# A sigmoid-attention and SwiGLU kernel: issue order from a list scheduler, scores in bursts of two, row tails loaded per batch, last stores on SyncE

## The chip, the cores and the metric

One core of one Trainium2 chip. The metric is the device time of one launch in microseconds (us). Faster or slower asks for 2%.

## The reference

```python
# q, k, v: (batch 8, heads 12, seq 448, head_dim 64)
scores = scale * np.matmul(q, k.transpose(0, 1, 3, 2)) - np.log(448)
attn = 1.0 / (1.0 + np.exp(-scores))          # a sigmoid, no softmax
x = np.matmul(attn, v)                        # -> (3584 tokens, 768)
g = x @ w_gate                                # 768 x 1536
silu = g * (1.0 / (1.0 + np.exp(-g)))
out = silu * (x @ w_val) @ w_out              # 1536 x 768
```

## The kernel before

Work is cut into 24 units of four heads of one batch; three units make a batch. A unit's attention is: transposes of q and k (`emit_tr`, twice), seven score products into double banks of PSUM with a sigmoid on ScalarE for each, and two PV products (`emit_pv`). The FFN runs three units behind: a block is a gate and a value product of six matmuls (`emit_f1`), and output products (`emit_f2`) come once two batches are through. The rows 384 to 447 of each head, the "row tails", are loaded apart. (PSUM is where the kernel has its matmuls write; PV is the product of the sigmoids with v.) Everything is issued in the order written; each engine works through its own queue in that order. The scores have two buffers (tag `A`), the transposes and output products share one (tag `TO`).

```python
def emit_sc(i, pp, s):                       # one score pair: two 64-row tiles side by side
    sc = psum.tile([128, 2, 512], FP32, tag="A", bufs=2, name="ps_sc")
    ...
# the loop over units i and four slots sl (cut)
if f1:
    gps = emit_f1(fb, ff, wg16, "ps_g")
    t1 = emit_gate_post(gps)
if sl == 0:
    jobs = [emit_sc(i, 0, 0), emit_sc(i, 0, 1)]
elif sl == 1:
    jobs = [emit_sc(i, 0, 2), emit_sct(i)]
elif sl == 2:
    jobs = [emit_sc(i, 1, 0), emit_sc(i, 1, 1)]
else:
    jobs = [emit_sc(i, 1, 2)]
...                                          # PV of (i-1, 1) in slot 0, of (i, 0) in slot 3
for jb in jobs:
    emit_sig(jb)
...
if i + 1 < NQ and sl in (1, 2):
    emit_tr(i + 1, sl - 1)
if f1:
    vps = emit_f1(fb, ff, wv16, "ps_v")
...                                          # then an output product, casts, loads
```

The loads of a unit bring q, k, v in 384 KB each and its tails in four small transfers of 256-byte rows; all stores are issued from GpSimd.

## Time and profile before

| before | |
|---|---|
| time, median | 479.8 us |
| TensorE busy | 95% of a span of 479.3 us |
| first score sigmoid starts | 10.98 us |
| 21st sigmoid starts (the last that three units need) | 32.16 us |
| first gate matmul starts | 34.42 us |
| last matmul starts / span ends | 473.0 / 479.3 us |

"Half clock" below is a stretch in which the profile's clock record grants TensorE 0.5, or in which matmuls start twice as far apart as later.

The prediction below shows the lines on TensorE. One view it only tells of is ScalarE's, in the timeline of the start (start and length in us, engine, line, what, count; in brackets the idle time before and what ended it):

```profile
19.28 2.80 ACT L188 ACTIVATE pt<-ps_sc,sbiast 128x896 f16<-128x896 f32 x3 [1.23 <-PE ps_sc L174]
...
22.85 5.63 ACT L188 ACTIVATE pt<-ps_sc,sbiast 128x896 f16<-128x896 f32 x6
...
30.37 4.75 ACT L188 ACTIVATE pt<-ps_sc,sbiast 128x896 f16<-128x896 f32 x5 [0.99 <-PE ps_sc L174]
```

Sigmoids run in rows of three to six without a hole, 0.93 to 0.95 us each (a row's length by its count). From the first to the 21st start 21.2 us pass, of which 20 at 0.935 us are 18.7: holes of 2.5 us in all (the idle times that the view prints add up to 2.6).

I also use one measure of my own. For each moment I take the time minus a fixed length for each matmul started until then: 187 ns for 448 columns, 160 ns for 384, 53 ns for a transpose, two half tiles side by side counted once. These are set just under the distances between starts in the full stretch, whose medians are 189, 162 and 56 ns. The result is TensorE time lost so far, whether to waits, to the half clock or to changes of tile mode.

### The profile page before, as it was taken

To read this page: it belongs to the slowest core of one execution; us is meant where nothing else is said; L and a number is where in the kernel's file an instruction comes from. 1 tells how busy PE (TensorE), PEld (TensorE's weight loads), DVE (VectorE), ACT (ScalarE), POOL (GpSimd) and SP (SyncE) were. 2 spreads that over 40 slices of the span, in tenths; PEclk is the share of its full clock that TensorE was granted. 3 is DMA by queue.
4 is the path that set the end of the run, shared out by engine and by line. 5 is a ranking of instruction groups with operands and counts; after the bars stand their busy time and mean duration, and the time that the engine had idled before them with its cause. 6 is when DMAs were issued, how large, how long until landed. Compare 5 with 4: busy or idle time off the path is not lost.

```text
span 479.3 us, 7353 instructions
## 1 busy us (share of the span) xinstructions
PE 455.2 (95%) x2832; PEld 223.6 (47%) x2832; DVE 207.1 (43%) x421; ACT 221.0 (46%) x295; POOL 125.0 (26%) x216
## 2 busy tenths in 40 slices
PE   2886999999999999999999999999999999999995
PEld 1332444444445544444444454454454544554562
DVE  3342555555444344444444445444544443433210
ACT  3883556566554445454554544454454462112110
POOL 2777677322130023311311033023210000000010
PEclk9997999999999999999999999999999999999998
DMA  8999999963414045144234033220000001010032
GB/s 233 307 340 327 330 333 332 260 182 106 115 52 133 0 149 148 42 142 115 82 100 117 34 120 92 85 83 36 33 2 33 34 34 33 21 46 34 33 100 98
DMA packets 68578, 58.67 MB, mean 122 GB/s; under 512 B 22208, under 2 KB 65216, under 8 KB 68544
## 3 DMA queue, kind: packets, MB, share of 16 engines
q1 hardware_dynamic: 66240, 47.20, 33.7%
q0 software_dynamic: 2304, 11.01, 6.3%
q8 instruction: 22, 0.36, 0.3%
q14 instruction: 12, 0.10, 0.1%
HBM read 47.19 MB, written 11.01 MB: 121 GB/s over the span
## 4 chain that ended last, share of the span: by engine, by line
PE 88%; DMA 6%; SPq 1%; issue 1%; DVE 1%; ACT 1%; POOL 0%; POOLq 0%
PE ps_g L218 23%; PE ps_v L218 22%; PE ps_o L250 16%; PE ps_ol L250 7%; PE ps_sc L174 7%; PE ps_pv L198 6%; PE ps_tr L153 3%; DMA st_k<-in_k_dram 3%; PE ps_pv L200 3%; PE ps_sct L182 2%; DMA st_wg<-in_moe_w_gate_dram 1%; DMA st_q<-in_q_dram 1%; DMA sv<-in_v_dram 1%; DVE t L226 1%; SPq L98 1%
## 5 line engine op out<-in xcount | busy, mean ns | idle before, releaser
L188 ACT ACTIVATE pt<-ps_sc,sbiast 128x896 f16<-128x896 f32 x144 | 138.7, 1004 | 2.5 <-PE ps_sc L174 2.5
L224 ACT ACTIVATE s<-ps_g 128x448 f16<-128x448 f32 x96 | 52.1, 543 | 168.7 <-PE ps_g L218 168.7
L218 PE MATMUL ps_g<-xT,wg 128*128 128x448 f16 x576 | 125.8, 355 | 0.8 <-DVE t L226 0.8
L218 PE MATMUL ps_v<-xT,wv 128*128 128x448 f16 x576 | 125.8, 355 | 0.0
L226 DVE TENSOR_TENSOR t<-ps_g,s 128x448 f16<-128x448 f32 x96 | 60.0, 625 | 148.2 <-ACT s L224 148.2
L250 PEld LDWEIGHTS <-hT 128*128 128x128 f16 x672 | 64.5, 98 | 48.2 <-DVE kbd L163 4.9
L218 PEld LDWEIGHTS <-wg 128*128 128x128 f16 x576 | 56.6, 98 | 52.8 <-issue 3.4
L250 PE MATMUL ps_o<-wo,hT 128*128 128x384 f16 x456 | 80.5, 327 | 0.0
L218 PEld LDWEIGHTS <-wv 128*128 128x128 f16 x576 | 54.9, 98 | 42.3 <-issue 1.3
L233 DVE SCALAR_TENSOR_TENSOR hT<-ps_v,t 128x448 f16<-128x448 f32 x96 | 60.0, 625 | 32.4 <-PE ps_v L218 28.8
L263 POOL DMA_DIRECT2D out_dram<-osb x24 | 13.2, 552 | 230.7 <-DVE osb L255 115.0
L174 PE MATMUL ps_sc<-qkT 64*128 64x448 bf16 x288 | 46.1, 368 | 2.9 <-ACT pt L188 2.6
L198 PE MATMUL ps_pv<-pt,v 128*64 128x448 f16 x288 | 37.0, 365 | 0.0
L250 PE MATMUL ps_ol<-wo,hT 128*128 128x384 f16 x216 | 35.9, 326 | 0.0
L160 DVE COPY qkT<-ps_tr 128x832 bf16<-128x832 bf16 x48 | 28.2, 588 | 17.0 <-PE ps_tr L156 17.0
L207 DVE CAST xT<-ps_pv 128x448 f16<-128x448 f32 x48 | 30.0, 625 | 12.7 <-PE ps_pv L200 11.0
L122 POOL CAST v<-st_v 128x768 f16<-128x768 f32 x24 | 19.8, 826 | 49.6 <-PE ps_pv L198 38.0
L153 PE MATMUL ps_tr<-idn,k 128*128 128x128 bf16 x144 | 17.0, 230 | 13.4 <-ACT k L120 6.2
L253 ACT ACTIVATE osb<-ps_o 128x384 f32<-128x384 f32 x19 | 9.3, 490 | 43.9 <-PE ps_o L250 43.9
L174 PEld LDWEIGHTS <-qkT 64*128 64x128 bf16 x288 | 10.8, 95 | 37.9 <-issue 37.5
L188 ACT ACTIVATE pt<-ps_sct,sbiast 128x896 f16<-128x896 f32 x24 | 24.2, 1010 | 0.1
L122 POOL CAST q<-st_q 128x768 bf16<-128x768 f32 x23 | 18.9, 823 | 19.0 <-issue 12.1
(36 smaller groups left out, 225.1 us busy)
## 6 DMA issues: line engine op xcount, KB each, us to landing
st_q<-in_q_dram SPq DMA_DIRECT2D x24, 384.0 KB, 4.8
st_k<-in_k_dram SPq DMA_DIRECT2D x24, 384.0 KB, 5.0
st_v<-in_v_dram SPq DMA_DIRECT2D x24, 384.0 KB, 4.0
out_dram<-osb POOLq DMA_DIRECT2D x24, 384.0 KB, 2.6
st_wg<-in_moe_w_gate_dram SPq DMA_DIRECT2D x12, 384.0 KB, 5.4
st_wv<-in_moe_w_val_dram SPq DMA_DIRECT2D x12, 384.0 KB, 6.5
st_wo<-in_moe_w_out_dram SPq DMA_DIRECT2D x12, 384.0 KB, 5.6
sqk<-in_q_dram SPq DMA_DIRECT2D x24, 64.0 KB, 3.3
```

What stands on the lines that cost most here:

```text
L122: eng.tensor_copy(out=o, in_=i)
L153: nc.tensor.transpose(out=ps[:, off + s * 128:off + (s + 1) * 128], in_=src[:, s, hs, :], identity=idn)
L160: nc.vector.tensor_copy(out=m, in_=ps[:, mo:mo + S + SM])
L174: nc.tensor.matmul(out=sc[:, hp, 0:S], lhsT=kT[r, s * 128:(s + 1) * 128], rhs=qT[r, :], start=True, stop=True)
L188: nc.scalar.activation(out=pt, in_=sc[:, :, 0:S], func=SIGM, bias=sb_t, scale=qkscale)
L198: nc.tensor.matmul(out=pv[c, :], lhsT=v16[i][:, 2 * pp + hp, s, :], rhs=pts[(i, pp, s)][:, hp, :], start=(s == 0), stop=False)
L207: nc.vector.tensor_copy(out=t, in_=pv)
L218: nc.tensor.matmul(out=ps, lhsT=w[c][:, j, ff * 128:(ff + 1) * 128], rhs=xT[(b, j)], start=(j == 0), stop=(j == KC - 1))
L224: nc.scalar.activation(out=s16, in_=gps, func=SIGM)
L226: nc.vector.tensor_tensor(out=t1, in0=gps, in1=s16, op=MULT)
L233: nc.vector.scalar_tensor_tensor(out=hT[(m, f)][:, o * S:(o + 1) * S], in0=vps, scalar=HSC, in1=t1, op0=MULT, op1=MULT)
L250: nc.tensor.matmul(out=o, lhsT=hT[(m, f)][:, t * 128:(t + 1) * 128], rhs=wo16[f][:, cs], start=(f == 0), stop=(f == NF - 1))
```

## The change

Its intent: fill TensorE's holes in the start by an order that knows when data come, and spend less on mode changes. Each step becomes an `Op` with an engine, an assumed duration, what it waits for, and buffers that it takes and gives. A list scheduler walks through assumed time and lets each engine take the first ready step among the next 40 (TensorE), 12, 16, 8 or 1; the program is then issued in order of the assumed starts. Below, the diff is cut and regrouped.

```diff
+LAT = {"PE": 0.2, "ACT": 0.1, "DVE": 0.08, "POOL": 0.12, "SP": 2.2}
+SWITCH = 0.1
+DMA_RATE = 330e3
+def list_schedule(ops, bufs, window):
 ...  (cut)
+            for o in q[:window.get(e, 1)]:
+                r = ready(o)          # None while a buffer that it takes isn't free
 ...
+    def burst(i, ds):
+        def fpe():
+            for pp, s in ds:
+                sc = psum.tile([128, 2, 512], FP32, tag="A", bufs=2, name="ps_sc")
 ...
+        a = op("PE", 0.19 * len(ds), fpe, deps=[R["qkT", i, pp] for pp, _ in ds],
+               mode=("R", "R"), take=["A"] * len(ds))
 ...
-                    jobs = [emit_sc(i, 0, 0), emit_sc(i, 0, 1)]
+                            burst(i, ((0, 0), (0, 1)))        # slot 0
-                    jobs = [emit_sc(i, 0, 2), emit_sct(i)]
+                        burst_tail(i)                         # slot 1
-                    jobs = [emit_sc(i, 1, 0), emit_sc(i, 1, 1)]
+                        burst(i, ((0, 2), (1, 0)))            # slot 2
-                    jobs = [emit_sc(i, 1, 2)]
+                        burst(i, ((1, 1), (1, 2)))            # slot 3
 ...
+            if (i + 3) % QB == 0:
+                tails_batch((i + 3) // QB)     # tails of three units in four transfers
 ...
+        dma = nc.sync if final else nc.gpsimd  # last stores; the very last one in halves,
+                                               # its eviction split over ScalarE and VectorE
+    window = {"PE": 40, "ACT": 12, "DVE": 16, "POOL": 8, "SP": 1}
+    for o in list_schedule(ops, slots, window):
+        o.fn()
```

A dummy activation loads the sigmoid table at once, unit 0's q, k and v are loaded and cast in halves, and FFN blocks are dealt out three per unit at first and up to five later. The matmuls are the same.

## The prediction

> **What bounds the kernel now.** I read the page first, parts 1 and 2: which engine is full, and where along the span it isn't.
>
> ```profile
> PE 455.2 (95%) x2832; PEld 223.6 (47%) x2832; DVE 207.1 (43%) x421; ACT 221.0 (46%) x295; POOL 125.0 (26%) x216
> ...
> PE   2886999999999999999999999999999999999995
> ...
> ACT  3883556566554445454554544454454462112110
> ...
> PEclk9997999999999999999999999999999999999998
> DMA  8999999963414045144234033220000001010032
> ```
>
> A slice is 12 us. From slice 4 (48 us) to the end TensorE is full, and no other engine is. Only three things can shorten the run: the first 48 us, less TensorE time for the same products, and the last microseconds after TensorE. In the first slices ACT is full in slices 1 and 2, and the DMA engines are full in slices 1 to 7, so those two limit the start.
>
> Next, the timeline of the start (start, length, engine, line, what; in brackets the idle time and what ended it):
>
> ```profile
> 9.68 1.28 ACT L188 ACT_TABLE_LOAD   x1 [3.49 <-PE ps_sc L174]
> 10.98 2.80 ACT L188 ACTIVATE pt<-ps_sc,sbiast 128x896 f16<-128x896 f32 x3
> ...
> 34.42 1.30 PE L218 MATMUL ps_g<-xT,wg 128*128 128x448 f16 x6
> ...
> 40.80 0.50 PE L153 MATMUL ps_tr<-idn,k 128*128 128x128 bf16 x3 [4.30 <-POOL k L122]
> ...
> 41.52 2.45 PE L218 MATMUL ps_v<-xT,wv 128*128 128x448 f16 x6
> ...
> 47.20 1.30 PE L218 MATMUL ps_v<-xT,wv 128*128 128x448 f16 x6
> ```
>
> The reader is to see four losses. The first score sigmoid runs at 10.98, after a table load that waited for the scores. The first FFN block starts at 34.42, when the 21 sigmoids of three units are through (ACT from 10.98 to 33.2, with about 1.5 us of holes: it paces this stretch). Then TensorE stands 4.30 us, because the next instruction in program order is a transpose of unit 4, whose k has only just been loaded and cast, while products for unit 3 and the FFN were to be had. And after that hole it runs at half clock: 2.45 us for six matmuls, later 1.30.
>
> Then the steady state, TensorE alone:
>
> ```profile
> 203.23 1.30 PE L218 MATMUL ps_g<-xT,wg 128*128 128x448 f16 x6
> 204.46 0.36 PE L174 MATMUL ps_sc<-qkT 64*128 64x448 bf16 x2
> 204.76 0.55 PE L182 MATMUL ps_sct<-qkT,kbd 128*128 128x448 bf16 x2
> 205.14 0.33 PE L153 MATMUL ps_tr<-idn,k 128*128 128x128 bf16 x3
> ```
>
> Starts count here, not lengths. Six full matmuls take 1.14 from start to start (the chain of waits prints 1.14), but before a 64-row score pair they take 1.23; the pair, two matmuls side by side worth 0.19, takes 0.30 until the full-array tail score. A change between full array and half tiles costs about 0.10 us each time. Per unit I count 4 entries into scores, 2 exits to full array, 2 from scores to the column-tiled PV, 2 from there to full array: 10 changes, about 1.1 us.
>
> Last, the end:
>
> ```profile
> 443.59 1.29 PE L218 MATMUL ps_g<-xT,wg 128*128 128x448 f16 x6 [0.16 <-DVE t L226]
> ...
> 473.42 0.56 DVE L255 TENSOR_SCALAR osb<-ps_ol 128x384 f32<-128x384 f32 x1 [3.34 <-PE ps_ol L250]
> ...
> 474.53 0.54 POOL L263 DMA_DIRECT2D out_dram<-osb  x1 [3.35 <-issue]
> ```
>
> Late FFN blocks with nothing between them wait 0.16 us per gate or value bank. After the last matmul 0.56 us of scaling, 0.55 us until the store's descriptor starts on GpSimd, 0.54 us of issue, and a landing (2.6 us in the table of DMA issues) make up the end at 479.3.
>
> **What the Trainium skill says.** "TensorEngine Tiling (Array Packing)", Key Properties: changing the tiling mode drains TensorE. The trace agrees, with the 0.10 us per change above. "TensorE: Matmul & The Clock Gate", Part 1: the clock falls to half after an idle window of about 3.4 us and comes back after a busy one of that length. The trace agrees: a 4.30 us hole, then 2.24 us per six matmuls in the chain for 4.5 us, then 1.14. "ScalarE: Activation LUTs", What ACT_TABLE_LOAD costs: about 1283 ns plus a drain; here the load took 1.28 us and no drain of that size shows before the sigmoid at 10.98. "DMA: Bandwidth & Descriptors", Why small descriptors are slow: transfers in 256-byte pieces lose bandwidth. The row tails are such pieces; in the stretch 14 to 18 us, in which two units' tails move, the engines are 0.95 busy at 231 GB/s, against 340 to 360 when weights move.
>
> **The change part by part.** No arithmetic goes away; the matmuls are the same, so TensorE's own work stays.
>
> (a) Start. TensorE's work up to 46.14, when it is full and at full clock, at full-rate durations: transposes 9 x 0.41 = 3.7, score pairs 21 x 0.19 = 4.0, tail scores 4 x 0.38 = 1.5, PV 6 x 0.88 = 5.3, three FFN halves 3.4, mode changes about 3.5: 21.4 us. So 46.1 - 21.4 = 24.7 us are lost before it is full.
> After the change: the sigmoid table is loaded by a dummy activation at once (1.28 us off the path), and q and k of unit 0 come in halves. Against that the row tails of three units come ahead of it, 0.39 MB for q/k where the first unit needed 0.13, in 256-byte pieces. In the trace the first tails were cast at 6.08; I put the new ones 1 us later, so transposes at 7, copy 0.6, scores at 8.2, first sigmoid at 8.7 instead of 11.0. Then 21 sigmoids at 0.94 (3 in 2.80) = 19.7 us plus the old 1.5 us of holes and 0.5 for bursts that need both score buffers: 30.4; PV and its cast 1.3: FFN from about 31.5 instead of 34.4. The 4.3 us hole and the half clock after it (2.3 us) should go, since the list order puts ready work first: three FFN blocks wait on the first weight chunk, whose casts ended at 26.7 in the trace. By 31.5 TensorE has done about 16.5 us of work, so 15 are lost. Gain 9.5 us. DMA check: 330 GB/s bring units 0-2, chunk 0, unit 3, chunk 1, unit 4 (11.8 MB) at about 38 to 41 us; work then in hand (3 blocks of 2.27, unit 3 of 4.9) lasts until 43. It is close, so I allow 1 us of waits: **-8.5 us**.
>
> (b) Three score bursts of two instead of 2, 1, 2, 1. One entry and one exit fewer per unit, 0.2 us, in 21 units past the start: 4.2 us, if the list order keeps PV behind its burst. If it separates them, one change comes back per burst and nothing is gained. I take **-3 us**.
>
> (c) Order in the steady state. The page has 14 waits of the output product's weight load on the key-block copy, 4.9 us together, some 0.13 us of it visible in the matmul starts each time (1.27 instead of 1.14 before ps_o): 2 us. The late bank waits: about 1 us. The scheduler may fill half: **-1.5 us**.
>
> (d) Stores. The last evictions are split over ACT and DVE (0.56 to about 0.35), the last store is halved and issued from SyncE, which drops the 0.55 us before the descriptor: **-1 us**. Of the other stores nothing is on the path. Fewer tail DMAs (24 x 4 to 8 x 4 issues of 0.6 us) free SyncE, but the DMA engines were full in the start anyway: 0.
>
> Sum: -14 us. 479.8 - 14 = **465.8 us**, 2.9% faster.
>
> **The rivals.** First: DMA is the true bound up to 96 us, and the earlier FFN start only meets the weights earlier. For: 1.02 to 1.12 DMA share from 20 us on, and the 4.3 us hole ended with a load. Against: TensorE had no hole from 46 us on, though it did four FFN blocks per unit with loads in the same order; the new order asks for three. If true, half of (a) is lost: about 470. Second: the static order is a queue, and where the schedule's durations differ from the chip's (it assumes 330 GB/s from the first byte, and no half clock) TensorE waits at the head for something late while ready work stands behind it. Each wait over 3.4 us costs clock as well. Likely in the first 50 us only; it would give 468 to 473. Third: two scores per burst need both score buffers, so ACT runs dry between bursts. In the steady state ACT needs about 10 us of a unit's 14 to 20, so it has room; in the start it would cost about 0.4 us per burst, 9 bursts, part of which I took. Fourth, the other way: filling TensorE with the next unit's scores and PV brings the start's loss to 10 us, total about 460.
>
> **Range and chances.** The start carries most of the spread (gain 3 to 13 us), the bursts 0 to 4.5, the rest 1 to 4. Taken together 458 to 473. The 2% line is 470.2 us; only when the start gives less than 4 or 5 us is it missed. Faster 0.80, within 2% 0.18, slower 0.02.
>
> **What would show it.** First sigmoid at 8 to 9.5 us; first gate matmul at 30 to 33; no TensorE hole over 3 us after it and full granted clock from there; TensorE full from then to the end. Per unit three score entries and eight mode changes, 13.8 us per unit with four FFN blocks and no output product, against 13.97 now. The end 1 us nearer to the last matmul. Wrong if the transposes or the gate still wait on casts of late loads after 31 us, if PV stands apart from its burst everywhere, or if new waits on score buffers cut into the full stretch.

## The result, and the profile after

The changed kernel takes 474.28 us (median of 4, 474.1 to 474.78) beside 479.8 us for the kernel before (4 runs); the ratio is 0.9886 with an interval from 0.9869 to 0.9904. It is 1.1% faster, within 2%, where 2.9% was foretold.

The page of the changed kernel, busy times and slices (11.8 us each):

```profile
PE 451.4 (96%) x2832; PEld 224.0 (47%) x2832; DVE 205.1 (43%) x422; ACT 221.9 (47%) x296; POOL 120.5 (26%) x207
...
PE   2778999999999999999999999999999999999996
...
ACT  3577666656445354453554455445545344121111
...
PEclk9979999999999999999999999999999999999999
DMA  8999999989413253332541323000000001110032
```

Against the page of before, TensorE's first four digits are 2, 7, 7, 8 as against 2, 8, 8, 6: the start is hardly better filled. ScalarE, which was at 8 in slices 1 and 2, is at 5 and 7. The half clock is still there, one slice earlier.

ScalarE's timeline in the start:

```profile
8.96 1.91 ACT L385 ACTIVATE pt<-ps_sc,sbiast 128x896 f16<-128x896 f32 x2 [4.58 <-PE ps_sc L362]
12.87 1.01 ACT L385 ACTIVATE pt<-ps_sct,sbiast 128x896 f16<-128x896 f32 x1 [2.00 <-PE ps_sct L376]
15.12 1.91 ACT L385 ACTIVATE pt<-ps_sc,sbiast 128x896 f16<-128x896 f32 x2 [1.24 <-PE ps_sc L362]
18.80 1.91 ACT L385 ACTIVATE pt<-ps_sc,sbiast 128x896 f16<-128x896 f32 x2 [1.77 <-PE ps_sc L362]
21.89 1.91 ACT L385 ACTIVATE pt<-ps_sc,sbiast 128x896 f16<-128x896 f32 x2 [1.19 <-PE ps_sc L362]
...
32.54 1.01 ACT L385 ACTIVATE pt<-ps_sct,sbiast 128x896 f16<-128x896 f32 x1 [2.12 <-PE ps_sct L376]
```

The first sigmoid is 2 us earlier, as foretold (8.96, foretold 8.7). Then they come in twos, with a hole of 1.2 to 2.1 us before most of them, each ended by a score product. The 21st starts at 37.90: 28.9 us after the first, with 10.2 us of holes where there had been 2.5.

TensorE's timeline:

```profile
30.83 0.50 PE L336 MATMUL ps_tr<-idn,k 128*128 128x128 bf16 x3 [0.80 <-POOL k L199]
...
31.55 0.95 PE L376 MATMUL ps_sct<-qkT,kbd 128*128 128x448 bf16 x2
...
40.51 1.30 PE L424 MATMUL ps_g<-xT,wg 128*128 128x448 f16 x6
```

The first gate comes at 40.51, not at 31.5, and 6 us later than before the change. The clock was halved again from 30.3 to 37.1 us: three transposes take 0.50, later 0.34.

By my measure, in us:

| kernel (its profiled run) | first sigmoid | 21st | first gate | lost at 46.2 | lost 46.2 to 400 | lost 400 to last | last matmul to end |
|---|---|---|---|---|---|---|---|
| before | 10.98 | 32.16 | 34.42 | 29.4 | 28.6 | 2.8 | 6.3 |
| changed | 8.96 | 37.90 | 40.51 | 28.3 | 24.1 | 3.3 | 4.2 |

So the start gave 1.1 us, the full stretch 4.5, the late blocks took back 0.5 and the end gave 2.1: 7.2 us between the two spans of 479.3 and 472.0. The medians differ by 5.5. The profiled run of before was 481.07 us, 1.3 above its median, so the start's true share may be nearer to nothing. (How a gate that is 6 us late can go with no more loss at 46.2: up to the first gate 27.8 us are lost where it was 22.1, but from the gate to 46.2 only 0.5 where it was 7.3. The 4.30 us hole and the half clock behind it, which came after the gate, are gone.)

### The profile page after: what moved, and what is told of

It reads as the page before. It is cut to its first block, busy times and chain, and to the rows that moved or that the text cites. A ratio compares the mean times of both kernels' runs of the same rounds, so it can differ in the third digit from the quotient of the medians.

```text
span 472.0 us, 7257 instructions
## 1 busy us (share of the span) xinstructions
PE 451.4 (96%) x2832; PEld 224.0 (47%) x2832; DVE 205.1 (43%) x422; ACT 221.9 (47%) x296; POOL 120.5 (26%) x207
## 4 chain that ended last, share of the span: by engine, by line
PE 88%; DMA 7%; SPq 1%; DVE 1%; ACT 1%; POOL 0%; issue 0%
PE ps_g L424 23%; PE ps_v L424 22%; PE ps_o L472 18%; PE ps_sc L362 6%; PE ps_pv L398 6%; PE ps_ol L472 5%; PE ps_tr L336 3%; PE ps_pv L400 3%; DMA st_v<-in_v_dram 3%; DMA st_k<-in_k_dram 2%; DMA st_wv<-in_moe_w_val_dram 2%; PE ps_sct L376 2%; DVE t L434 1%; SPq L239 1%; ACT s L430 1%; PE ps_tr L338 0%
## 5 line engine op out<-in xcount | busy, mean ns | idle before, releaser
L385 ACT ACTIVATE pt<-ps_sc,sbiast 128x896 f16<-128x896 f32 x144 | 136.8, 1006 | 34.1 <-PE ps_sc L362 34.1
L472 PE MATMUL ps_o<-wo,hT 128*128 128x384 f16 x516 | 90.9, 326 | 0.0
L472 PEld LDWEIGHTS <-hT 128*128 128x128 f16 x672 | 65.6, 98 | 45.8 <-issue 0.7
L362 PE MATMUL ps_sc<-qkT 64*128 64x448 bf16 x288 | 42.3, 369 | 4.3 <-ACT pt L385 3.6
L199 POOL CAST v<-st_v 128x768 f16<-128x768 f32 (+1 forms) x25 | 20.2, 808 | 67.8 <-PE ps_pv L398 63.0
L497 POOL DMA_DIRECT2D out_dram<-osb x15 | 8.3, 556 | 100.0 <-DVE osb L485 53.0
L483 ACT ACTIVATE osb<-ps_o 128x384 f32<-128x384 f32 x22 | 10.8, 491 | 40.7 <-PE ps_o L472 40.7
L472 PE MATMUL ps_ol<-wo,hT 128*128 128x384 f16 x156 | 26.8, 326 | 0.0
L385 ACT ACTIVATE pt<-ps_sct,sbiast 128x896 f16<-128x896 f32 x24 | 24.1, 1003 | 4.2 <-PE ps_sct L376 4.1
L485 DVE TENSOR_SCALAR osb<-ps_o 128x384 f32<-128x384 f32 x21 | 11.7, 558 | 27.3 <-PE ps_o L472 27.3
```

The source lines that it names most:

```text
L199: nc.gpsimd.tensor_copy(out=o, in_=i)
L362: nc.tensor.matmul(out=sc[:, hp, 0:S], lhsT=kT[r, s * 128:(s + 1) * 128], rhs=qT[r, :], start=True, stop=True)
L385: nc.scalar.activation(out=pt, in_=T[("sc",) + key][:, :, 0:S], func=SIGM, bias=sb_t, scale=qkscale)
L472: nc.tensor.matmul(out=o, lhsT=T["hT", m, f][:, t * 128:(t + 1) * 128], rhs=wo16[f][:, cs], start=(f == 0), stop=(f == NF - 1))
```

## The experiments

Twelve kernels, each edited from the changed one unless said otherwise, each run with three timed rounds beside the kernel before (478 to 482 us in all of them), all correct. Runs 1 to 4, 5 to 7, 8 to 10, and 11 and 12 were each taken on one chip; across these groups the ratios compare better than the medians.

**1. Single score pairs in the start.** Theory A: a burst of two is one step that takes two of two score buffers, so it is ready only when ScalarE has emptied both. From the scheduler's own constants its period is then 0.38 + 0.1 for the burst and the change, 0.2 until ScalarE may start, two sigmoids of 0.95 and 0.1 until the buffer is free: about 2.7 us for 1.9 us of ScalarE's time. Meanwhile transposes and PV are put into TensorE's queue ahead of it.

```diff
     def burst(i, ds):
+        if len(ds) > 1 and i < QB:
+            for d in ds:
+                burst(i, (d,))
+            return
```

> Score bursts of units 0 to 2 given to the scheduler as single score pairs, each needing one score buffer; bursts of two from unit 3 on. Theory A (an indivisible burst of two needs both of the two score buffers, so ScalarE runs dry between bursts in the start): ScalarE's holes before the first gate shrink from about 10 us to 3 or less, first gate matmul at 33 to 35 us instead of 40.5, time 467 to 470 us. Theory B (row tails batched at the front and before unit 3 delay the data): first gate no earlier than 39, time 473 to 475. Theory C (the DMA engines bound the stretch up to 96 us whatever the order): first gate earlier, but TensorE holes appear after it and the time stays at 472 or more.

Measured: 468.94 us (467.76 to 469.68), ratio 0.9768 [0.9743, 0.9793]. ScalarE and the first gate:

```profile
15.23 1.91 ACT L389 ACTIVATE pt<-ps_sc,sbiast 128x896 f16<-128x896 f32 x2 [0.33 <-PE ps_sc L366]
17.85 2.81 ACT L389 ACTIVATE pt<-ps_sc,sbiast 128x896 f16<-128x896 f32 x3 [0.71 <-PE ps_sc L366]
...
21.58 5.60 ACT L389 ACTIVATE pt<-ps_sc,sbiast 128x896 f16<-128x896 f32 x6
...
28.11 3.80 ACT L389 ACTIVATE pt<-ps_sc,sbiast 128x896 f16<-128x896 f32 x4
```
```profile
34.00 1.31 PE L428 MATMUL ps_g<-xT,wg 128*128 128x448 f16 x6
```

The sigmoids stand in rows again. The 21st starts at 30.90 instead of 37.90, holes are 3.6 us instead of 10.2, the gate comes 6.5 us earlier, and 23.1 us are lost at 46.2 instead of 28.3. From there on the two kernels lose the same, 24.1 us up to 400. Theory A holds (its holes of "3 or less" came to 3.6), and theory C falls: after the gate at 34 no matmul waits for the cast of a load (weight loads do three times, 0.6 us at most), so the DMA engines, though full, don't bound this. The clock differs too in this run: it is up from 16.7 us, not from 20.1, and doesn't fall at 30. What the run changes is only the order, so it doesn't split the 5.3 us between the missing scores, the late casts that the work put ahead of them waits for, and the clock.

**2. Row tails per unit.** The tails loaded unit by unit with the small buffers of before (edit: `tails_batch(b)` becomes `tails_qk(i)` and `tails_v(i)`, called among the loads of each unit).

> Row tails loaded per unit as before the change, all else as changed. Theory A: first gate 39 to 41, time 473 to 475 us. Theory B: unit 3's casts end 1.5 to 2 us earlier, no wait at the transposes near 30 us, the clock stays full, first gate at 36 to 37, time 469 to 471 us.

Measured: 475.35 us (474.28 to 475.93), ratio 0.9897. The time lies just above theory A's range and far above theory B's; yet both have a part. The first sigmoid comes at 7.29 instead of 8.96 and the gate at 38.37; 26.6 us are lost at 46.2, 1.7 less than in the changed kernel. But it is given back: 27.3 us are lost from there to 400 instead of 24.1. TensorE's waits from 46 us on:

```profile
PE ps_tr L338 <- POOL k L199: 3.2, 3, 1.4
PE ps_g L426 <- DVE t L436: 1.1, 7, 0.2
```

The first line isn't there in the changed kernel: three waits of transposes for casts, 3.2 us together, two of 1.4 us at 66 and 78 us. Batching the tails costs the first unit 1.3 to 1.7 us (its first sigmoid is at 8.62 to 8.96 in the changed kernel and in runs 5 and 7) and saves about 3 later. By its time it is not what was missing. But the start isn't a clean test: in this run the clock came up only at 28.4 us (PV at 25.41 still takes 1.33 us), against 20.1 in the changed kernel, so how much the tails alone give there stays open.

**3. Four bursts, 2, 1, 2, 1, scheduled.**

```diff
-                        burst_tail(i)
+                        burst(i, ((0, 2),))
+                        burst_tail(i)
-                        burst(i, ((0, 2), (1, 0)))
+                        burst(i, ((1, 0), (1, 1)))
-                        burst(i, ((1, 1), (1, 2)))
+                        burst(i, ((1, 2),))
```

> Scores of a unit in four bursts 2, 1, 2, 1 as before the change, each burst indivisible for the scheduler, all else as changed. Theory A: the single pairs let ScalarE run on, start 2 to 4 us shorter; but 1 more entry and exit per unit costs up to 0.2 us in 21 units, 4 us back: time 473 to 476 us with a first gate at 36 to 38. If the bursts did not matter at all: 474, first gate 40.5.

Measured: 478.07 us (476.2 to 479.76), ratio 0.9956: 2 us more than expected. The gate is at 38.82, so the start gains 0.8 us of lost time, less than the 2 to 4 expected. The full stretch loses 29.2 us instead of 24.1. Counted in the matmul records of that stretch, successive matmuls change their tile mode 205 times here, 173 times in the changed kernel and 204 times before. At the 0.10 us of the prediction 32 changes are 3.2 us of the 5.1. Transposes that wait for casts, at 68 and 79 us, add 1.4; the changed kernel has no such wait.

**4. Program order.** The changed kernel's steps issued as written.

```diff
-    for o in list_schedule(ops, slots, window):
+    for o in ops:
```

> The changed kernel issued in the order in which its steps are written, without the list scheduler. If the scheduler's order is what gains in the full stretch: 478 us or more, with long holes in the start as before the change. If the order is worth nothing: 474.

Measured: 479.31 us (478.47 to 483.44), ratio 0.9999 [0.9955, 1.0044]. The order is worth 5 us, and not in the start (27.7 us lost at 46.2, 28.3 with the scheduler) but after it: 29.0 us instead of 24.1. There are only 159 mode changes in that stretch, 14 fewer than with the scheduler and 45 fewer than before, so the bursts alone should have gained over the kernel before. They don't. From 120 to 400 us the view of waits has, for the output products:

```profile
PEld L472 <- DVE kbd L348: 8.3, 16, 0.6
...
PE ps_o L472 <- DVE kbd L348: 1.5, 8, 0.2
```

The product waits for VectorE to empty the bank that it shares with the transposes. Before the change it was 4.9 us, 14 times, on the weight load and nothing on the matmuls; with the scheduler neither line is there. From the starts, value blocks followed by an output product lose 4.0 us over the run, 1.1 before and nothing with the scheduler. So in the full stretch neither part works alone: scheduled with four bursts or unscheduled with three, it loses 29 us, as the kernel before; both together save 4.5.

**5. A filler for the clock.** Six useless matmuls ahead of each score burst of units 0 to 3.

```diff
         def fpe():
+            if i <= QB:
+                w = psum.tile([128, S], FP32, tag="G", bufs=2, name="ps_w")
+                for _ in range(6):
+                    nc.tensor.matmul(out=w[:, 0:128], lhsT=idn, rhs=idn, start=True, stop=True)
             for pp, s in ds:
```

> The changed kernel with six 128x128 matmuls of no use ahead of every score burst of units 0 to 3, into a bank that nothing else uses then, so that TensorE's clock stays up in the start; the schedule is the same. If the half clock from 30.3 to 37.1 us is a cause of its own: full clock by 16 us and none lost at 30, first gate at 36.5 to 38, time 470.5 to 472.5 us. If ScalarE's starving alone sets the start: the clock is full but the first gate stays at 39.5 to 41 and the time at 473.5 to 475.

Measured: 477.36 us (476.08 to 477.89), ratio 0.9927. The clock stayed full at 30 us, as in run 1, and the gate came at 40.78, not earlier. But it's no clean test: a cast was later here and cost 2 us by 17 us, and 72 extra matmuls, 0.056 us apart at best, are about 4 us of work, some of it in unit 3 after the gate. The time is longer than either theory expected.

**6. Single pairs, unit 0's second halves earlier.** As 1, with q's and k's second halves loaded ahead of the v tails and that k cast on ScalarE.

```diff
-    load_main(0, "v", v, 0)
-    for nm, src in (("q", q), ("k", k), ("v", v)):
+    for nm, src in (("q", q), ("k", k)):
         load_main(0, nm, src, 1)
+    load_main(0, "v", v, 0)
+    vtails_batch(0)
+    load_main(0, "v", v, 1)
-    cast_main(0, "k16", "POOL", BF16, 1)
+    cast_main(0, "k16", "ACT", BF16, 1)
```

> Single score pairs in units 0 to 2, and the second halves of unit 0's q and k loaded ahead of the row tails of v, its k cast on ScalarE. Theory A with what is left of ScalarE's holes put down to the second half of unit 0 (2.48 us before the tail score): first gate at 31.5 to 33 us instead of 34.0, time 466 to 468. If the next bound is the load of unit 3: first gate at 33.5 or more, time 468 to 469.

Measured: 469.28 us (467.87 to 470.82), ratio 0.9764: a miss, no gain over 1. The hole before the tail score shrank from 2.48 to 0.88 us, but holes of 1.84 and 2.21 us came before unit 1's scores and tail: TensorE was at half clock until about 22 us (a PV there takes 1.33 us, in 1 it takes 0.76 by then).

**7. Last stores on GpSimd.**

```diff
-        eng = "SP" if final else "POOL"
-        dma = nc.sync if final else nc.gpsimd
+        eng = "POOL"
+        dma = nc.gpsimd
```

> The changed kernel with the last stores issued from GpSimd again, the split of the last eviction and store kept. Expected from the two traces (6.3 us from the last matmul to the end before, 4.2 after): 1 to 2 us longer, 475.3 to 476.3. If the halving of the last store gives the gain: 474.5 or less.

Measured: 476.83 us (476.12 to 477.26), ratio 0.9919. From the last matmul to the end it is 6.0 us, 4.2 with SyncE: 1.8 us, and the halving of the last store with the split eviction gives the 0.3 left to the 6.3 of before. The median is 2.5 us above that of the changed kernel, but the kernel before was slower on this chip too (480.74); by the ratios, 0.9919 and 0.9886, it is 1.6 us, about what the stores cost. The start of this profiled run lost 29.4 us with the same order there. So runs of one order can differ by a microsecond in the start.

**8. The filler in units 1 and 2 only.** As 5, with `if i in (1, 2)`.

> As the filler run, but the six useless matmuls stand ahead of the score bursts of units 1 and 2 only, so that the first 14 us and unit 3 are left as they are. If the half clock from 30.3 to 37.1 us costs time of its own: clock full there, first gate at 37.5 to 39 us instead of 40.5, time 471 to 473. If ScalarE's waits for whole bursts set the start alone: first gate at 40 to 41, time 474 to 475.5.

Measured: 474.82 us (474.21 to 475.42), ratio 0.9893, gate at 41.36. The clock fell at 31.4 us again, but for 3.4 us instead of 6.8. Time and gate didn't move with it. With 5 this speaks against the half clock at 30 us as a cause of its own, and so as the cause of run 1's gain, but neither run took it away cleanly.

**9. Single pairs, early halves, warm clock.** As 6, with 56 useless matmuls while TensorE waits for the first data (26 before the first transpose, 18 before the tail's, 6 after each half).

> Single score pairs in units 0 to 2, the second halves of unit 0's q and k loaded early, and 56 useless matmuls while TensorE waits for the first data, so that its clock is up from about 8 us instead of 22. If the half clock in the first 22 us is what left holes of 1.84 and 2.21 us on ScalarE in the run without them: first gate at 31.5 to 33.5 us, time 465.5 to 467.5. If not: 35, 469.

Measured: 471.27 us (469.81 to 471.9), ratio 0.9814 [0.9784, 0.9844], unclear by the 2% rule: no gain, and rather slower than without them (0.9764 [0.9728, 0.98]). The clock was up at 5 us, and the 21st sigmoid started at 28.96, 1.5 us of holes in all, just what the prediction had hoped for. Yet the gate came at 35.81:

```profile
28.50 0.36 PE L378 MATMUL ps_sc<-qkT 64*128 64x448 bf16 x2
31.94 0.41 PE L344 MATMUL ps_tr<-idn,k 128*128 128x128 bf16 x3 [3.08 <-POOL k L199]
32.15 0.53 PE L344 MATMUL ps_tr<-idn,q 128*128 128x128 bf16 x3
32.47 0.31 PE L348 MATMUL ps_tr<-idn,qk 128*128 128x128 bf16 x1
32.71 1.33 PE L414 MATMUL ps_pv<-pt,v 128*64 128x448 f16 x6
```

The head of the queue is a transpose of unit 3, whose k was cast only then. PV of unit 2, which needs nothing more, stands behind it for 3 us, and the clock falls just after the hole, at 32.1 us. This is the 4.30 us hole of the kernel before in another place: the order is static, and it had counted on an earlier load.

**10. As 1, warm clock.** Loads as in the changed kernel.

> Single score pairs in units 0 to 2 and the same useless matmuls before the first data, loads as in the changed kernel. Holes on ScalarE of 2.5 us before the tail score of unit 0 stay (they wait for a cast), the others shrink: first gate at 33 to 34 us instead of 34.0, time 467.5 to 469.

Measured: 469.58 us (468.87 to 469.85), ratio 0.9781; gate at 34.47, expected 33 to 34; the time too lies just outside what was expected, and its verdict is unclear. The clock came up and fell again from 10.3 to 17.1 us, in the waits for unit 0's second half. A warm start that the data can't follow is no gain.

**11 and 12. As 9 and as 6, with the scheduler told a lower rate**, so that it puts PV of unit 2 ahead of unit 3's transposes.

```diff
-DMA_RATE = 330e3
+DMA_RATE = 280e3
```

> As the run with single pairs, early loads and a warm clock, but the scheduler is told 280 instead of 330 GB/s, so that the transposes of unit 3 come after both PV of unit 2 in TensorE's queue, not before. In that run the 21st sigmoid began at 28.96 us, yet the first gate came at 35.81 behind a 3.08 us wait of unit 3's transposes for their cast. If that place in the queue is what is left of the start: first gate at 31 to 32.5 us, no wait over 1 us before it, time 466 to 468.5. If the rest of the order suffers from the false rate as much: 469 or more with an early gate.

> The same without the useless matmuls: clock at half until about 20 us, so first gate at 33.5 to 35 us, time 467 to 469.5; the difference to the run with them is what the cold clock costs in the start, 1 to 3 us if it costs anything on the path.

Measured: 468.15 us (466.03 to 469.86), ratio 0.9754 [0.9706, 0.9801], for 11, and 468.03 us (467.58 to 469.48), ratio 0.9759 [0.9729, 0.979], for 12. Run 11 on TensorE:

```profile
18.31 1.33 PE L414 MATMUL ps_pv<-pt,v 128*64 128x448 f16 x6
...
32.65 0.36 PE L416 MATMUL ps_pv<-pt,vbd 128*128 128x448 f16 x1
32.84 1.30 PE L440 MATMUL ps_g<-xT,wg 128*128 128x448 f16 x6
33.98 0.33 PE L344 MATMUL ps_tr<-idn,k 128*128 128x128 bf16 x3
```

In 11 no wait for a cast of unit 3 over 0.2 us is left and the gate comes at 32.84 us, the earliest of all, though later than the 31 to 32.5 expected; in 12 it comes at 34.14, inside its range. The place in the queue was what held 9 back: from the 21st sigmoid to the gate 6.9 us pass in 9 and 1.6 in 11. The warm clock didn't last in 11, though: it fell from 14.4 to 21.2 us (the PV above at half clock), holes of 1.29 and 2.20 us on ScalarE are back, and the 21st sigmoid is at 31.27, not at 28.96. So 11 against 12, 1.3 us at the gate and nothing in the time, doesn't measure what a cold clock costs, and no run has both the clock of 9 and the order of 11. Runs 1, 11 and 12 can't be told apart: all are about 2.4% faster than the kernel before (11's interval just crosses the 2% line, so its verdict is unclear) and some 5 to 6 us faster than the changed one. Run 1 is the smallest edit.

## Why the prediction was wrong

**What bounds the kernel** held: TensorE full from 48 us on, ScalarE pacing the sigmoids of three units before that.

**(a), the start, -8.5 us, is the step that failed.** It came to about -1.1. The term that was mis-sized is "21 sigmoids at 0.94" with "the old 1.5 us of holes and 0.5 for bursts that need both score buffers". The first sigmoid came as foretold. The holes were 10.2 us, not 2.0 (the old ones were misread too: 2.5 us, not 1.5). So up to the first gate 27.8 us were lost, 5.7 more than before, where a gate 2.9 us earlier had been foretold. The third rival had named the cause (bursts that need both buffers let ScalarE run dry), but put 0.4 us on each of 9 bursts, about the time of a burst on TensorE, and took 0.5 of that sum of 3.6. What counts is when the order lets the burst begin. The scheduler holds it ready only with both buffers empty, and by then has given TensorE transposes and PV, at half clock, some waiting for casts. Taking that away in units 0 to 2 (run 1) moved the gate from 40.5 to 34.0 and the time by 5.3 us, of the 8.5 us by which the prediction missed.
The other 2 to 3 us: after run 1 the gate was at 34.0, not 31.5. Runs 6, 9 and 11 show two more things in that place, TensorE's half clock up to about 20 us and unit 3's transposes at the head of the queue. Run 9 mended the clock, run 11 the queue. Together they might bring the gate to about 30.5 us, an estimate from 9's 21st sigmoid at 28.96 and the 1.6 us that follow it in 11; no run shows it, and an earlier gate in 11 than in 1 didn't shorten the time measurably. How much of the rest each holds stays open.
"The 4.3 us hole and the half clock after it" did go from behind the gate: the loss from there to 46.2 fell from 7.3 to 0.5 us. But a half clock of 6.8 us came ahead of the gate, without a long hole.

**(b) and (c), -3 and -1.5 us,** together came to -4.5 in the stretch from 46 to 400 us. There 31 mode changes fewer are 3.1 of it by the 0.10 us each, an estimate (8.4 changes a unit, where 8 were foretold for 10), and the waits for the shared bank 1.1. Late waits for gate banks grew instead of shrinking, 0.5 us the other way. That "the scheduler may fill half" of the waits for the shared bank was too low a share of too high a sum: it removed all, but they were 1.1 us and not 2. The two parts need each other, which I hadn't seen: runs 3 and 4 have one part each and gain nothing there.

**(d), -1 us,** was -2.1 in the trace; run 7 puts 1.8 on SyncE.

**The rivals.** DMA as the true bound: no, after the earlier gate of run 1 no matmul waited for a load. The static queue: yes, but it cost most only once ScalarE was fed (run 9). The range of 458 to 473 missed the 474.28 narrowly because three of its four terms were right or low, and the largest was nearly all gone.

## What to carry to other kernels

Making two steps one for a scheduler changes when they may start: here a burst that takes all buffers of a ring starved their consumer in the start, where the consumer set the pace. In the full stretch, where TensorE did, the bursts showed no such loss. Find out which engine paces each stage, and be wary of merging where it is the consumer. In a static order ask what stands at the head of each queue when a load is late, and let work that needs no load go first.

## What the Trainium skill lacked or had wrong

- "TensorE: Matmul & The Clock Gate", Part 1, puts the fall to half clock after an idle window of about 3.4 us. In the changed kernel it fell at 30.3 us, for 6.8 us, with no idle of more than 0.87 us in the seven us before; by these records TensorE was busy 3.07 and 2.60 us of the 4 us from 22 and from 26 us. Run 1, only a little denser there (3.17 and 2.74), didn't fall. The page doesn't say how much work in a window is enough. The fourteen traces do, by my measure: the times between changes of the clock are multiples of 3.41 us, and on that grid, up to the last matmul, the clock fell after each of the nine stretches whose matmuls' fixed lengths sum to at most 33% (33% in the changed kernel, 38% in run 1) and after none with 34% or more.
- The same page: full clock after about 3.4 us of busy time. Before the change TensorE had no hole of over 0.1 us from 12.9 us on, and starts stood at half clock until 19.2 us; in run 2 it was 80 to 86% busy from 14.7 to 25 us and the clock came up only at 28.4. This doesn't contradict the page, which has the window run free, but shows how full it has to be. The clock record begins with the first rise, and until then the profile's clock row shows full clock. So in the first stretch the distance of matmul starts has to be read, not the row; no page has this.
- "TensorEngine Tiling (Array Packing)", Key Properties, has the drain at a change of tiling mode but no figure: 0.10 us each way here, some 24 us of the kernel before (an estimate, 239 changes).
- "ScalarE: Activation LUTs", What ACT_TABLE_LOAD costs, adds a drain of about 1380 ns to the load. Here the load took 1.28 us and the next activation started 0.02 us after it (2.03 us); ScalarE had done nothing before, so this case has nothing to drain ahead of the load.
- No page weighs the two sides of batching loads, a later first arrival against fewer waits afterwards, with a number: tails of three units in one go delayed the first sigmoid by 1.3 to 1.7 us and spared 3.2 us of waits after 46 us (run 2).
